# Chunked attention before a mixture of experts: value rows loaded once, 24 rows of each value window copied on chip

## The chip, the cores and the metric

One core of a Trainium2 chip runs the whole program. The metric is the device time in microseconds, from the first to the last instruction of a run; lower is better. The profile is one execution recorded by the hardware profiler; its engines are called PE (TensorE, the matrix engine), DVE (VectorE), ACT (ScalarE), POOL (GpSimd) and SP (the engine that does nothing here but issue loads).

## What is computed

The reference is attention over short windows, followed by a layer of experts of which each token uses one:

```python
B, H, S, D = q.shape                      # 4, 8, 768, 64
chunk, left_ctx, right_ctx = (32, 16, 8)
for c in range(S // chunk):               # 24 chunks
    l_start = max(0, c * chunk - left_ctx)
    r_end = min(S, c * chunk + chunk + right_ctx)
    k_full = np.concatenate([mem_k, k[:, :, l_start:r_end]], axis=2)    # 8 memory rows, up to 56 of the sequence
    v_full = np.concatenate([mem_v, v[:, :, l_start:r_end]], axis=2)
    a = softmax(scale * q_c @ k_full.T)
    out[:, :, c * chunk:c * chunk + chunk] = a @ v_full
x = out.transpose(0, 2, 1, 3).reshape(B * S, H * D)
# gate: each token's expert of 8 and its probability; then
out[mask] = gate_w[mask, None] * (np.maximum(x[mask] @ w1[e], 0) @ w2[e])
```

Consecutive windows overlap: a window has 56 rows of the sequence and the next one starts 32 rows further on, so 24 rows of each window are also in the one before it.

## The kernel before

**Units.** The attention goes through 16 units of two heads each (`NU`), and each unit in two halves of 12 chunks (`hf`). One pass of the loop at L731 is one half unit: it computes the scores of its half (`scores`, L273), the products with the values of the half before (`attend`, L306), and the transposes of the finished half before that (`trans_x`, L328). `trans_k`, `regroup_q` (L228, a VectorE copy of q) and `store_k` (L265) for unit u+1 stand in the first half of unit u, `trans_q` in the second; the values of unit u+1 are first used in the second half of unit u+1, one pass after its first scores.

**The tiles.** `kbds` (two of them) hold the keys of a unit, 64 columns to a chunk and head: 8 memory keys written by `mem_keys` (L247, GpSimd; the first units on VectorE) and 56 of the sequence written by `store_k`. `vws` (three of them, `NVW`) hold the values: partition 64 h + r is row r of the window of head h, the free dimension is chunk, head and 64 + 1 columns. The extra column is 1 for rows that count, so that its product is the softmax's denominator; rows outside the sequence have 0 there, from `vmask`. The tiles are blanked once at the start (`blank_v`, L205, L208, L210).

**The loads.** All loads of q, k and v are issued by SP, in the order of the program: `load_qk` (L96) three units ahead and `load_v` (L219 to L223) two units ahead, at the end of the first half of a unit. A value load may start when the products that used the same tile three units before are done. Per head there are four loads: memory rows for all 24 chunks (rows 0 to 7), 56 rows for the 22 inner chunks, 40 rows for the first and 48 for the last. Each moves rows of 64 numbers, 256 B.

**Other queues.** Instructions of TensorE, SP and GpSimd run in the order of the program. GpSimd has the memory keys, the store of each finished unit to the tensor `xd` (L333, a DMA), the store of the gates (L497), and some one-hot rows of the routing (L558, L560: tiles 0 and 1 of batches 0, 1 and 2). The routing of a batch of tokens (`route`) is cut into small steps that `pump` puts between the attention's instructions; TensorE multiplies the one-hot rows (L568) at its place in the order. After the last unit, the weights of the experts stream in (`load_w`, L600, L604), are split into two parts (`conv`, L607, L608) and multiplied (L650, L662).

Of the kernel before, what the change touches and what calls it, by code (L numbers as in the profile page):

```python
# [48 lines left out]
def tile_chunk_attention_top1_moe(  # L49
# [47 lines left out]

    # the tensor engine's clock comes up while the first loads are on their way
    idle = const.tile([P, 640], BF16, name="idle")
# [10 lines left out]

    # ---------------------------------------------------------------- constants
    kbds = [pers.tile([P, NCH, 2, 64], F32, name=f"kbd{i}") for i in range(2)]
# [28 lines left out]
    nc.gpsimd.iota(iota_i, [[1, 192]], base=0, channel_multiplier=0)  # L141
    # rows of a value window that lie outside the sequence
    kcol = const.tile([P, 1], F32, name="kcol")
# [3 lines left out]
    mtmp = const.tile([P, 1], F32, name="mtmp")  # L147
    nc.gpsimd.tensor_scalar(vmask[:, 0:1], kcol, 23.5, None, op0=ALU.is_gt)
    nc.gpsimd.tensor_scalar(mtmp, kcol, 7.5, None, op0=ALU.is_lt)
    nc.gpsimd.tensor_add(vmask[:, 0:1], vmask[:, 0:1], mtmp)  # L150
    nc.gpsimd.tensor_scalar(vmask[:, 1:2], kcol, 55.5, None, op0=ALU.is_lt)

# [21 lines left out]
    def more_constants():  # L174
        nc.vector.tensor_copy(iota, iota_i)
        nc.vector.tensor_scalar(rev[:, 0], iota[:, 0:E], -1.0, float(E), op0=ALU.mult, op1=ALU.add)
        nc.vector.memset(ones_b, 1.0)
        nc.vector.tensor_scalar(tri_b, iota[:, 0:P], pcol, None, op0=ALU.is_gt)
        # EMPTY less the token number, and its negative, for token T*128+p
        nc.vector.tensor_scalar(tokn, iota[:, 0:N // P], float(P), pcol, op0=ALU.mult, op1=ALU.add)  # L180
        nc.vector.tensor_scalar(tokn, tokn, -EMPTY, None, op0=ALU.add)
        nc.vector.tensor_scalar(tokm, tokn, -1.0, None, op0=ALU.mult)
        nc.vector.memset(table, EMPTY)
        nc.vector.tensor_scalar(tail_row, pcol[0:64], 31.5, None, op0=ALU.is_gt)
        nc.vector.tensor_scalar(col0, iota[0:64, 0:E], float(HI), None, op0=ALU.mult)
        nc.vector.memset(tot, 0.0)
        nc.vector.tensor_copy(mod_f, mod_i[:, :, 0])
    def bias_rows():
        # of each token
        modT = bank()  # L190
        nc.tensor.transpose(modT[:, 0:N // P], mod_f, ident[0:N // P, 0:N // P])
        mt = const.tile([P, N // P, 1], F32, name="mt")
        m0 = const.tile([P, N // P, 1], F32, name="m0")
        nc.vector.tensor_copy(mt[:, :, 0], modT[:, 0:N // P])
        nc.vector.tensor_scalar(m0, mt, -1.0, 1.0, op0=ALU.mult, op1=ALU.add)
        bsh = [P, N // P, E]
        b1t = pers.tile(bsh, F32, name="b1t")
        nc.vector.tensor_tensor(btok, m0.to_broadcast(bsh), bias_b[:, 0:1, :].to_broadcast(bsh), op=ALU.mult)
        nc.vector.tensor_tensor(b1t, mt.to_broadcast(bsh), bias_b[:, 1:2, :].to_broadcast(bsh), op=ALU.mult)
        nc.vector.tensor_add(btok, btok, b1t)  # L200

    # ---------------------------------------------------------------- attention
    def blank_v(i):
# [10 lines left out]
    def load_v(u):  # L214
        vw = vws[u % NVW]
        for h in range(2):
            hh = 2 * u + h
            r0 = 64 * h
            nc.sync.dma_start(vw[r0:r0 + NMEM, :, h, 0:D], mvf[hh].unsqueeze(1).to_broadcast([NMEM, NCH, D]))  # L219
            src = bass.AP(tensor=vf.tensor, offset=(hh * S + 16) * D, ap=[[D, 56], [32 * D, NCH - 2], [1, D]])  # L220
            nc.sync.dma_start(vw[r0 + NMEM:r0 + 64, 1:NCH - 1, h, 0:D], src)
            nc.sync.dma_start(vw[r0 + 24:r0 + 64, 0, h, 0:D], vf[hh * S:hh * S + 40])
            nc.sync.dma_start(vw[r0 + NMEM:r0 + 56, NCH - 1, h, 0:D], vf[hh * S + 720:hh * S + S])  # L223

# [19 lines left out]
    def mem_keys(u, eng):  # L244
        for h in range(2):
            r = slice(64 * h, 64 * h + 64)
            eng.tensor_copy(kbds[u % 2][r, :, h, 0:NMEM], memT[r, u:u + 1, :].to_broadcast([64, NCH, NMEM]))  # L247

    def trans_k(u):
        k2 = k2s.pop(u)  # L250
        for h in (1, 0):
            hh = 2 * u + h
            t = kts[u, h] = bank()
            for i in range(3):
                nc.tensor.transpose(t[:, 8 + i * P:8 + (i + 1) * P], k2[:, 3 * h + i, :], ident)
            # memory keys stand where the first and last windows pass the sequence's ends
            pads = bass.AP(tensor=t.tensor, offset=t.offset, ap=[list(t.ap[0]), [392, 2], [1, 8]])
            mem_sel = ident[:, 4 * hh:4 * hh + 4].unsqueeze(1).unsqueeze(1)
            nc.tensor.matmul(pads, mkp, mem_sel.to_broadcast([P, 2, 2, 4]), start=True, stop=True)  # L259

    def store_k(u, h, j, copy):
        tt = kts[u, h][64 * j:64 * j + 64]
        win = bass.AP(tensor=tt.tensor, offset=tt.offset, ap=[list(tt.ap[0]), [16, NCH], [1, 28]])
        dst = kbds[u % 2][64 * h:64 * h + 64, :, h, NMEM:64]
        copy(dst.rearrange("p c (i j) -> p c i j", j=2)[:, :, :, j], win)  # L265
# [68 lines left out]

    # the routing of a batch goes on between the instructions of the attention
    routing, now = [], [0]
# [15 lines left out]

    # ---------------------------------------------------------------- routing, in stages
    plan = {}
# [11 lines left out]
    def plan_row(pos, tail, pt, nfull):  # L366
        """For the slot that stands at pos: its expert, whether that is new, its first column of the table."""
        vec = nc.vector
# [8 lines left out]
        if tail is not None:  # L377
# [5 lines left out]
            vec.tensor_add(three[:, 2], three[:, 2], c)  # L383
            # a tail that follows a slot of its own expert
            vec.tensor_tensor(same, pos, nfull, op=ALU.is_equal)
# [7 lines left out]
    def plan_slots():  # L393
        """Slots of 256 tokens of one expert, those of expert ohg first."""
        vec = nc.vector
# [5 lines left out]
        vec.tensor_tensor_scan(end, oth, oth, ng, op0=ALU.add, op1=ALU.bypass)  # L401
        # first slot and the one behind the last; of expert ohg, 0 and its number of slots
        vec.tensor_sub(sta, end, oth)
# [7 lines left out]
    def plan_tails():  # L411
        """Behind the slots, tails of up to 128 against the order of the experts, that of expert ohg last.

        Row p of regs holds slot p for p < 32, tail p - 32 from there on."""
        vec = nc.vector
# [20 lines left out]
    def route(b):  # L436
# [24 lines left out]
        yield "v"  # L461
        # first expert of those with the largest logit
        eq = sm.tile(sh, F32, name="eq")
# [12 lines left out]
        yield "pe"  # L476
        # rank of each token within its expert, and the counts
        rkb = bank()
# [7 lines left out]
        nc.tensor.matmul(rkf[:, 0:NT * E], tri_b, oh.rearrange("p t e -> p (t e)"), start=False, stop=True)  # L486
        # gate
        sx = sm.tile([P, NT, 1], F32, name="sx")
# [28 lines left out]
        if b == B - 2:  # L517
            # the expert with the most tokens so far has at least one full slot
            cm = sm.tile([P, 1], F32, name="cm")
# [19 lines left out]
        if b == B - 1:  # L539
            nc.vector.tensor_copy(plan_new("counts"), rk[0:64, NT, :])  # L540
            yield "v"
        # where the token goes: row lo, column ac of the table
        hot = []
# [33 lines left out]

    # ---------------------------------------------------------------- experts
    raw, wh, wl = [None] * 16, [None] * 16, [None] * 16
# [65 lines left out]
    def mm1(f):  # L645
        ph = bank()[:, 0:256]
        # what waits for the lower part of x comes last
        for n in range(12):
# [25 lines left out]

    # the same for up to 128 tokens, whose products have the tokens on the partitions
    def tail_mm1(half):
# [27 lines left out]

    # ---------------------------------------------------------------- the run
    for i in range(NVW):
# [16 lines left out]
    for i in range(1, NVW):  # L723
        load_v(i)

    units = [(u, hf) for u in range(NU) for hf in range(2)]
# [4 lines left out]
    for i in range(n + 2):  # L731
# [12 lines left out]
        if u + 1 < NU and hf == 0:  # L744
# [10 lines left out]
            pump(1)  # L755
        elif u + 1 < NU:
            trans_q(u + 1)
            store_q(u + 1, 0)
            store_q(u + 1, 1)
            exps(u, hf)  # L760
            pump(3)
        elif live:
            exps(u, hf)
            pump(3)
# [34 lines left out]
        if (u, hf) == (NU - 2, 1):  # L799
# [13 lines left out]
            gather(0)  # L813
            # the later weights wait for the gather to be under way
            for f in range(NFIRST, 8):
# [126 lines left out]
```

## Time and profile before

| | |
|---|---|
| runs (three) | median 504.73 us, 500.7 to 508.09 |
| the profiled execution | span 505.4 us, mean granted TensorE clock 0.954 |
| busy over the span | PE 454.4 us, DVE 335.7, ACT 296.1, POOL 145.9 |
| DMA | 104448 packets, 64.48 MB; 53851 packets under 512 B |
| first product with values to the last | 22.3 to 170.6 us |
| first weights of the experts issued | 161.8 us |

How to read it: rows of busy time by window give, after the window and its length, the busy time of PE, PEld (TensorE's weight load), DVE, ACT and POOL with the number of instructions in brackets, then the granted TensorE clock, the share of time the 16 DMA engines were busy on average, and the GB/s moved. Rows in order of time give start and duration in us, the engine, the line, the operation with its tiles, and in square brackets how long the engine sat idle and what ended that. Groups of instructions give the total busy time in us and the mean in ns, then the idle time before them. Rows of waits give the total, the number and the longest. DMA issues give KB for one DMA.

### The profile page before, as it was taken

To read this page: it belongs to the slowest core of one execution; us is meant where nothing else is said; L and a number is where in the kernel's file an instruction comes from. 1 tells how busy PE (TensorE), PEld (TensorE's weight loads), DVE (VectorE), ACT (ScalarE), POOL (GpSimd) and SP (SyncE) were. 2 spreads that over 40 slices of the span, in tenths; PEclk is the share of its full clock that TensorE was granted. 3 is DMA by queue.
4 is the path that set the end of the run, shared out by engine and by line. 5 is a ranking of instruction groups with operands and counts; after the bars stand their busy time and mean duration, and the time that the engine had idled before them with its cause. 6 is when DMAs were issued, how large, how long until landed. Compare 5 with 4: busy or idle time off the path is not lost. (4 is left out here: it accounts for less than half of the span.)

```text
span 505.4 us, 12069 instructions
## 1 busy us (share of the span) xinstructions
PE 454.4 (90%) x4093; PEld 387.5 (77%) x4093; DVE 335.7 (66%) x760; ACT 296.1 (59%) x588; POOL 145.9 (29%) x238
## 2 busy tenths in 40 slices
PE   6769878796788779899999999999999999999892
PEld 3657666585666568889898989898898989897672
DVE  7756675584768597576865758484756657575593
ACT  5457674583655655546465656464655656565682
POOL 8112115114215582403051625343030303030100
PEclk8699997897999998999999999999999999999897
DMA  8999989989999921202031368771111202020830
GB/s 176 167 214 181 204 170 211 213 178 177 185 212 188 330 89 22 86 22 83 2 99 29 106 169 272 231 243 64 43 58 28 84 1 85 1 85 5 263 117 10
DMA packets 104448, 64.48 MB, mean 128 GB/s; under 512 B 53851, under 2 KB 95027, under 8 KB 104372
## 3 DMA queue, kind: packets, MB, share of 16 engines
q1 hardware_dynamic: 96512, 41.76, 38.9%
q0 software_dynamic: 6720, 21.62, 14.0%
q8 instruction: 36, 0.59, 0.5%
q14 instruction: 40, 0.33, 0.2%
q10 hardware_dynamic: 1140, 0.18, 0.2%
HBM read 97.05 MB, written 13.16 MB: 218 GB/s over the span
## 5 line engine op out<-in xcount | busy, mean ns | idle before, releaser
L650 PEld LDWEIGHTS tr<-xt,w 128*128 128x128 f32 x1152 | 141.2, 193 | 2.4 <-issue 0.6
L650 PE MATMUL tr<-xt,w 128*128 128x256 f32 x1152 | 142.7, 285 | 0.2 <-DVE h L652 0.2
L608 DVE TENSOR_TENSOR wl<-raw,wh 128x512 fp32r<-128x512 f32 x107 | 76.7, 727 | 13.9 <-ACT wh L607 5.9
L608 DVE TENSOR_TENSOR w<-raw,w 128x512 fp32r<-128x512 f32 x115 | 72.5, 686 | 0.0
L667 POOL DMA_INDIRECT out_dram<-o,ix_now x24 | 24.3, 1013 | 165.3 <-ACT o L666 161.6
L662 PE MATMUL av<-wh,h 128*128 128x512 f32 x208 | 69.9, 402 | 0.0
L662 PE MATMUL sc<-wh,h 128*128 128x512 f32 x208 | 69.7, 402 | 0.0
L607 ACT CAST w<-raw 128x512 fp32r<-128x512 f32 x120 | 66.9, 625 | 4.5 <-DMA raw<-in_moe_w_dram 4.5
L607 ACT CAST wh<-raw 128x512 fp32r<-128x512 f32 x112 | 67.2, 613 | 2.4 <-DVEq L907 2.2
L651 ACT ACTIVATE h<-tr 128x256 fp32r<-128x256 f32 x96 | 36.6, 383 | 48.3 <-PE tr L650 31.8
L652 DVE SCALAR_TENSOR_TENSOR h<-tr,h 128x256 fp32r<-128x256 f32 x96 | 40.7, 424 | 35.3 <-ACT h L651 35.2
L642 ACT CAST xt<-tr 128x512 fp32r<-128x512 f32 x26 | 15.1, 587 | 68.8 <-PE tr L640 46.6
L643 DVE TENSOR_TENSOR xt<-tr,xt 128x512 fp32r<-128x512 f32 x26 | 17.8, 692 | 52.9 <-ACT xt L642 52.9
L306 PE MATMUL av<-vw,PT 128*32 128x130 f32 x768 | 32.1, 295 | 17.8 <-DMA k<-in_k_dram 7.5
L662 PEld LDWEIGHTS av<-wh,h 128*128 128x128 f32 x208 | 39.2, 189 | 9.1 <-DVE h L703 0.4
L662 PEld LDWEIGHTS sc<-wh,h 128*128 128x128 f32 x208 | 39.0, 188 | 9.1 <-DVE h L703 0.4
L265 ACT COPY kbd<-tr 64x672 f32<-64x672 f32 x47 | 36.2, 769 | 15.1 <-PE tr L259 14.6
L662 PE MATMUL av<-wl,h 128*128 128x512 f32 x104 | 41.0, 394 | 0.0
L662 PE MATMUL sc<-wl,h 128*128 128x512 f32 x104 | 40.9, 393 | 0.0
L306 PEld LDWEIGHTS av<-vw,PT 128*32 128x32 f32 x768 | 23.0, 116 | 21.7 <-issue 11.6
L333 POOL DMA_DIRECT2D xd<-xb x16 | 14.0, 876 | 73.8 <-DVE l L453 29.8
L273 PE MATMUL sc<-kbd,qT 128*32 128x128 f32 x768 | 30.1, 294 | 4.5 <-DVE kbd L265 4.5
(206 smaller groups left out, 645.8 us busy)
## 6 DMA issues: line engine op xcount, KB each, us to landing
raw<-in_moe_w_dram SPq DMA_DIRECT2D x240, 256.0 KB
vw<-in_v_dram SPq DMA_DIRECT2D x32, 308.0 KB
k<-in_k_dram SPq DMA_DIRECT2D x16, 384.0 KB
q<-in_q_dram SPq DMA_DIRECT2D x16, 384.0 KB
xd<-xb POOLq DMA_DIRECT2D x16, 384.0 KB, 6.7
vw<-in_mem_v_dram SPq DMA_DIRECT2D x32, 48.0 KB
vw<-in_v_dram SPq DMA_DIRECT2D x32, 10.0 KB
vw<-in_v_dram SPq DMA_DIRECT2D x32, 12.0 KB
```

Of the source, the lines that this page charges most:

```text
L265: copy(dst.rearrange("p c (i j) -> p c i j", j=2)[:, :, :, j], win)
L273: nc.tensor.matmul(sc[32 * j:32 * j + 32, t * P:(t + 1) * P], qT[:, 32 * c:32 * c + 32], kbd[:, c].rearrange("p h m -> p (h m)"), start=Tr ...
L306: nc.tensor.matmul(avb[32 * j:32 * j + 32, t * W:(t + 1) * W], PT[:, t * P + 32 * j:t * P + 32 * j + 32], vw[:, c].rearrange("p h d -> p ( ...
L607: nc.scalar.copy(wh[i], raw[i])
L608: (eng or nc.vector).tensor_sub(wl[i], raw[i], wh[i].bitcast(F32))
L642: nc.scalar.copy(xth[:, sl], t)
L643: nc.vector.tensor_sub(xtl[:, sl], t, xth[:, sl].bitcast(F32))
L650: nc.tensor.matmul(ph, w[f][:, c * P:(c + 1) * P], x[:, c, :], start=(n == 0), stop=(n == 11))
L651: nc.scalar.activation(hh[:, f], ph, AF.Relu)
L652: nc.vector.scalar_tensor_tensor(hl[:, f], ph, 0.0, hh[:, f].bitcast(F32), op0=ALU.max, op1=ALU.subtract)
L662: nc.tensor.matmul(pos[t], x, w[8 + f], start=(f == 0 and n == 0), stop=(f == 7 and n == 2))
L667: return nc.gpsimd.indirect_dma_start(out=out, out_offset=bass.IndirectOffsetOnAxis(ap=ix, axis=0), in_=o, in_offset=None, bounds_check=N ...
```

## The change

The order of the rows in a window is turned round: rows 0 to 55 are the sequence, 56 to 63 the memory (keys and values alike, masks accordingly). Of the sequence, `load_v` loads only what the chunk before does not have: rows 24 to 55 of chunks 0 to 22, rows 24 to 47 of the last chunk, and rows 16 to 23 of the first. The memory rows are loaded last of the four instead of first. Rows 0 to 23 of chunks 1 to 23 are copied by GpSimd from rows 32 to 55 of the chunk before, in the same tile: one copy a head (`share_v`), 24 partitions by 23 x 64 numbers. These copies stand behind the first value loads for unit 0, and for unit u+1 at the start of the second half of unit u, ahead of `trans_q`.

```diff
-    nc.gpsimd.tensor_scalar(vmask[:, 0:1], kcol, 23.5, None, op0=ALU.is_gt)
-    nc.gpsimd.tensor_scalar(mtmp, kcol, 7.5, None, op0=ALU.is_lt)
-    nc.gpsimd.tensor_add(vmask[:, 0:1], vmask[:, 0:1], mtmp)
-    nc.gpsimd.tensor_scalar(vmask[:, 1:2], kcol, 55.5, None, op0=ALU.is_lt)
+    nc.gpsimd.tensor_scalar(vmask[:, 0:1], kcol, 15.5, None, op0=ALU.is_gt)
+    nc.gpsimd.tensor_scalar(vmask[:, 1:2], kcol, 47.5, None, op0=ALU.is_lt)
+    nc.gpsimd.tensor_scalar(mtmp, kcol, 55.5, None, op0=ALU.is_gt)
+    nc.gpsimd.tensor_add(vmask[:, 1:2], vmask[:, 1:2], mtmp)
...
-            nc.sync.dma_start(vw[r0:r0 + NMEM, :, h, 0:D], mvf[hh].unsqueeze(1).to_broadcast([NMEM, NCH, D]))
-            src = bass.AP(tensor=vf.tensor, offset=(hh * S + 16) * D, ap=[[D, 56], [32 * D, NCH - 2], [1, D]])
-            nc.sync.dma_start(vw[r0 + NMEM:r0 + 64, 1:NCH - 1, h, 0:D], src)
-            nc.sync.dma_start(vw[r0 + 24:r0 + 64, 0, h, 0:D], vf[hh * S:hh * S + 40])
-            nc.sync.dma_start(vw[r0 + NMEM:r0 + 56, NCH - 1, h, 0:D], vf[hh * S + 720:hh * S + S])
+            src = bass.AP(tensor=vf.tensor, offset=(hh * S + 8) * D, ap=[[D, 32], [32 * D, NCH - 1], [1, D]])
+            nc.sync.dma_start(vw[r0 + 24:r0 + 56, 0:NCH - 1, h, 0:D], src)
+            nc.sync.dma_start(vw[r0 + 24:r0 + 48, NCH - 1, h, 0:D], vf[hh * S + S - 24:hh * S + S])
+            nc.sync.dma_start(vw[r0 + 16:r0 + 24, 0, h, 0:D], vf[hh * S:hh * S + 8])
+            nc.sync.dma_start(vw[r0 + 56:r0 + 64, :, h, 0:D], mvf[hh].unsqueeze(1).to_broadcast([NMEM, NCH, D]))
+
+    def share_v(u):
+        vw = vws[u % NVW]
+        for h in range(2):
+            r0 = 64 * h
+            nc.gpsimd.tensor_copy(vw[r0:r0 + 24, 1:NCH, h, 0:D], vw[r0 + 32:r0 + 56, 0:NCH - 1, h, 0:D])
...
-            eng.tensor_copy(kbds[u % 2][r, :, h, 0:NMEM], memT[r, u:u + 1, :].to_broadcast([64, NCH, NMEM]))
+            eng.tensor_copy(kbds[u % 2][r, :, h, 56:64], memT[r, u:u + 1, :].to_broadcast([64, NCH, NMEM]))
...
-        dst = kbds[u % 2][64 * h:64 * h + 64, :, h, NMEM:64]
+        dst = kbds[u % 2][64 * h:64 * h + 64, :, h, 0:56]
...
     for i in range(1, NVW):
         load_v(i)
+    share_v(0)
...
         elif u + 1 < NU:
+            share_v(u + 1)
             trans_q(u + 1)
```

## The prediction

> **What bounds the kernel now.** The page first, to see in which stage the edited lines run and what is full there.
>
> ```profile
> span 505.4 us, 12069 instructions
> ...
> PEclk8699997897999998999999999999999999999897
> DMA  8999989989999921202031368771111202020830
> ```
>
> Forty slices of 12.6 us. DMA is at 8 or 9 tenths for the first fourteen (to about 175 us: the attention) and mostly below 4 behind; in those slices the granted clock dips too. Next the busy times by window: the whole attention loop, then three short stretches.
>
> ```profile
> 16.00:171.00 155.00, 129.12 (x2084) 101.78 (x2076) 101.98 (x309) 95.80 (x184) 39.00 (x67) 0.92 1.01 198
> 33.00:36.00 3.00, 0.49 (x3) 0.52 (x4) 0.48 (x1) 0.00 (x0) 0.00 (x0) 0.91 1.16 304
> 38.00:42.00 4.00, 4.00 (x77) 3.02 (x72) 2.34 (x6) 2.99 (x6) 1.48 (x3) 0.89 0.80 106
> ```
>
> Over the loop the DMA share is 1.01, TensorE is busy 129.12 of 155 us, VectorE 101.98, GpSimd 39.00. The stretch with q and k rows moves 304 GB/s; the one with value rows 106 GB/s, at a share of 0.80. Value rows are the slow traffic. Is the DMA stream what sets the pace? The SP queue in order of time:
>
> ```profile
> 42.80 0.43 SPq L96 DMA_DIRECT2D k<-in_k_dram  x1
> ...
> 44.37 1.59 SPq L221 DMA_DIRECT2D vw<-in_v_dram  x1
> 46.01 2.72 SPq L222 DMA_DIRECT2D vw<-in_v_dram  x1
> 48.78 0.33 SPq L223 DMA_DIRECT2D vw<-in_v_dram  x1
> ...
> 145.75 0.42 SPq L96 DMA_DIRECT2D k<-in_k_dram  x1
> ```
>
> SP issues without a gap, and a 10 KB load (L222) holds it 2.72 us behind the 308 KB load of L221: the stream is pushed back, and SP waits for room rather than for the compute engines. From unit 5's k (42.80) to unit 15's (145.75) are ten units: 10.30 us each. The compute engines need less. TensorE's score blocks, and the wait in the list that follows:
>
> ```profile
> 63.48 0.86 PE L273 MATMUL sc<-kbd,qT 128*32 128x128 f32 x24
> ...
> 67.69 0.86 PE L273 MATMUL sc<-kbd,qT 128*32 128x128 f32 x24
> ...
> 69.92 0.87 PE L306 MATMUL av<-vw,PT 128*32 128x130 f32 x24
> ...
> 71.40 0.86 PE L273 MATMUL sc<-kbd,qT 128*32 128x128 f32 x24
> ...
> 77.53 1.65 PE L306 MATMUL av<-vw,PT 128*32 128x130 f32 x24 [3.19 <-DMA k<-in_k_dram]
> ```
>
> Two unstalled half units take 4.21 and 3.71 us, 7.92 us a unit, routing included. Then comes a stall on a load, and the next block runs 1.65 us instead of the 0.87 us at 69.92. The sums of such waits in the loop:
>
> ```profile
> DVE qr L228 <- DMA q<-in_q_dram: 8.3, 4, 3.1
> ...
> PE av L306 <- DMA k<-in_k_dram: 7.5, 2, 4.3
> ...
> PE av L306 <- DMA vw<-in_v_dram: 5.6, 3, 2.7
> ```
>
> So the attention is paced by its loads; from 171 us on TensorE paces, and nothing there is edited.
>
> **The change, part by part.** The rows per load come from the DMA issues:
>
> ```profile
> vw<-in_v_dram SPq DMA_DIRECT2D x32, 308.0 KB
> k<-in_k_dram SPq DMA_DIRECT2D x16, 384.0 KB
> q<-in_q_dram SPq DMA_DIRECT2D x16, 384.0 KB
> xd<-xb POOLq DMA_DIRECT2D x16, 384.0 KB, 6.7
> vw<-in_mem_v_dram SPq DMA_DIRECT2D x32, 48.0 KB
> vw<-in_v_dram SPq DMA_DIRECT2D x32, 10.0 KB
> vw<-in_v_dram SPq DMA_DIRECT2D x32, 12.0 KB
> ```
>
> *Fewer value rows.* A value row is 256 B. A head now loads 1232 + 192 + 40 + 48 = 1512 of them; after the change 32 x 23 + 24 + 8 + 192 = 960, so a unit of two heads drops from 3024 to 1920, or 276 of its 756 KB. SP still issues four loads a head. Three prices for a unit:
> - By bytes: k, q, xd and values are 1908 KB a unit; 276 / 1908 x 10.30 = 1.5 us.
> - By packets, all alike: k, q and xd have 2304 of 512 B; 1104 / 5328 x 10.30 = 2.1 us.
> - By the stretches: at 304 GB/s the 1152 KB (1.18 MB) of k, q and xd take 3.9 us, the values the other 6.4 us; 1104 / 3024 of it is 2.3 us.
>
> I take 2.0 us, nearest to the packet price, because the 106 GB/s stretch shows that value rows cost more than their bytes. A loss is excluded: the same rows go to the same places, only fewer of them. The new DMA pace is 8.3 us, still above the 7.92 us of the engines. The ten units between the two quoted k issues gain, and with them the values of units 14 and 15, issued after 145.75; the first units meet a pipeline that is still filling, and I count nothing for them. 12 x 2.0 = 24 us.
>
> The Trainium skill, "DMA: Bandwidth & Descriptors", the paragraph "How many engines (k)", says that a DMA runs on the largest number up to 16 that divides its outer dimension. By it the 56-row load has 14 engines and the 32-row load 16, the memory rows 8 before and after. The busiest engine would fall from 382 to 290 packets a unit, an estimate of 7.8 us of DMA. No row here shows single engines; it would lead to the fourth rival below.
>
> *Two copies a unit on GpSimd* (24 partitions, 23 x 64 = 1472 elements). No row shows a copy that moves partitions. The nearest rows:
>
> ```profile
> L247 POOL COPY kbd<-memT 64x192 f32<-64x192 f32 x28 | 10.4, 372 | 8.3 <-PE sc L273 7.1
> L205 POOL MEMSET vw<- 128x3120 f32 x3 | 8.2, 2729 | 0.1
> L608 POOL TENSOR_TENSOR w<-raw,w 128x512 fp32r<-128x512 f32 x5 | 6.7, 1371 | 4.9 <-ACT w L607 4.9
> ...
> L333 POOL DMA_DIRECT2D xd<-xb x16 | 14.0, 876 | 73.8 <-DVE l L453 29.8 <-DVE table L569 11.3 <-DVE xb L321 11.1
> ```
>
> The memset's 0.875 ns an element gives 1.3 us, L608's 2.68 ns gives 3.9 us. L247 is the one plain copy: 372 less 192 x 0.875 leaves 0.2 us fixed. I take 0.2 + 1.3 = 1.5 us, 3.0 us a unit. GpSimd then does 3.0 + 2 x 0.37 + 0.88 = 4.6 of 8.3 us: hidden behind the loads. At 3.9 us it does 9.4 us: that cover is gone, and the pace is 9.4 instead of 8.3, 13 us of the 24 given back.
>
> *The new wait.* The copies of unit u+1 stand in GpSimd's queue at the start of the second half of unit u, and wait for its values to land. Behind them queue the xd store of unit u-1, the memory keys of unit u+2 (needed a unit later), and in the last unit the first gather of the experts' tokens. GpSimd's queue now, from its last one-hot rows to that gather:
>
> ```profile
> 156.82 1.16 POOL L560 TENSOR_SCALAR a<-iota,ac,tokm 128x192 fp32r<-128x192 f32 x1
> 157.94 0.94 POOL L333 DMA_DIRECT2D xd<-xb  x1
> 161.21 0.18 POOL L620 CAST ix<-table 128x2 int32 x1 [2.33 <-DVE table L569]
> ```
>
> The routing's one-hot rows stand ahead of the copies (the steps that issue them run a half unit earlier), so TensorE does not wait for them; the copies of unit 15 come between that one of 156.82 and the store at 157.94. Unit 15's last value load is the last of the stream:
>
> ```profile
> 160.64 0.33 SPq L223 DMA_DIRECT2D vw<-in_v_dram  x1
> ```
>
> With today's backlog the copies would end after about 161 + 3 = 164 us, and the gather, at 161.21 now, would be 3 us late. Where loads set the pace, values land just ahead of their product, and the copies put 3.0 us between; in the stream of units that is only an offset, since the loads of later units go on, and I see it once, at the end: 3 us. Between 0 (loads that have caught up) and 6 (offset and gather one after the other).
>
> *Start.* Unit 0's copies follow the value tiles' memsets and its loads. The value tile's list:
>
> ```profile
> L306 PE MATMUL av<-vw,PT x768: 270/274/427, 22.3 to 170.6; 128*32 128x130 f32 x192
> ...
> L208 POOL MEMSET vw<- x6: 135/138/431, 6.5 to 13.4; 64x24 f32 x6
> ```
>
> Between the last memset (13.4 us) and the first product (22.3) there is room for 3.0 us of copies, unless the loads land late. Nothing to 2 us; I take 1.
>
> *The port between VectorE and GpSimd.*
>
> ```profile
> 7.17 2.70 POOL L205 MEMSET vw<- 128x3120 f32 x1
> ...
> 7.39 2.60 DVE L175 CAST iota<-iota_i 128x192 f32<-128x192 int32 x1
> ```
>
> The one copy of each unit that has the form of this cast, from the loop's groups:
>
> ```profile
> L228 DVE COPY qr<-q 128x768 f32<-128x768 f32 x15 | 8.3, 554 | 8.3 <-DMA q<-in_q_dram 8.3
> ```
>
> A VectorE cast of 192 elements lasts until the memset on GpSimd is over, five times what a copy of 768 (L228) takes. Such a lock could hold VectorE up to two copies a unit, 3.0 us, at L228. VectorE is busy 101.98 / 155 x 10.30 = 6.8 us a unit: with a typical 0.7 us it stays below 8.3. I cost it at nothing; covered by the loads.
>
> The Trainium skill, "SBUF — State Buffer", section "Who interferes with whom", calls this port pair an exclusive lock that the engine which comes first holds for a whole instruction. The two rows above agree, 2.60 us against 2.70; it speaks against the change and is the first rival below.
>
> *Nothing:* the shift of memory keys and masks to other columns has the same instructions with the same shapes; memory rows last instead of first moves 48 KB behind 192 KB in the same queue, no more work.
>
> **Sum:** 505.4 - 24 + 3 + 1 = 485.4 us of span. The runs' median, 504.73, is 0.7 us below the profiled span; so 485 us, its own range 477 to 494.
>
> **Rivals.**
> - *VectorE becomes the bound.* If both copies are in its way in each unit, VectorE needs 6.8 + 3.0 = 9.8 us a unit: 12 x 0.5 = 6 us gained, 499. For it: the locked cast. Against: one SBUF-to-SBUF copy a unit, mostly at another time.
> - *Only the waits for value loads go.* The waits above put just 5.6 us at vw; if the rest of the loop's idle time has other causes, 505.4 - 5.6 + 4 - 0.7 = 503 us. For it: that list. Against: one queue carries all loads, and q and k stand in it behind values.
> - *Slower: the copy that moves partitions is dear.* Place: GpSimd's queue. GpSimd has 1.62 us of other work a unit, so it decides from (10.30 - 1.62) / 2 = 4.3 us a copy; at 5 us the pace is 11.6, 15 x 1.3 = 20 us lost, 525. For it: no row of its kind, and L608 already at 3.9. Against: L247.
> - *The loads stop being the bound.* DMA falls below 7.92 and the engines set the pace: 12 x 2.38 = 29 us, less 1 at the start: 477. For it: the 0.80 share in the value stretch, that is idle DMA engines. Against: no sign yet that the engines hold 7.92 through every unit.
>
> **How the numbers follow.** Forecast 0.54, VectorE 0.12, only the waits 0.12, dear copy 0.10, engines' pace 0.12. Two per cent, 10 us, is about what a measurement of this kernel can tell from no change (its runs spread from 500.7 to 508.09). Faster: 0.54 + 0.12 + 0.03 of VectorE's case = 0.69; same: 0.09 + 0.11 = 0.20; slower: 0.10 + 0.01 = 0.11. Range 473 to 508: from 4 us below the engines' pace, if the first units gain too, to a cheap gain with 4 us of cost behind it (503 and its spread of 4); the dear copy is left out.
>
> **What would show it.** Right: k issues about 8.3 us apart, stalls on k, q and vw loads nearly gone, copies near 1.5 us, the last attention product some 20 us earlier than 171, and the stages behind as long as now. Wrong: copies over 3 us; TensorE waiting for the GpSimd copies; VectorE's L228 at 2 us instead of 0.554; k issues still 10 us apart with a full DMA share, which would say that rows are not what the loads cost.

## The result and the profile after

The changed kernel takes 490.96 us (median of four runs, 488.23 to 491.6), the kernel before 504.67 us in the four runs beside it (500.7 to 508.09). The ratio is 0.973, 95% interval 0.967 to 0.979: faster by some 14 us. The profiled execution took 490.55 us.

The page of the changed kernel, the rows that answer to those of before:

```profile
span 488.8 us, 12153 instructions
...
PEclk9799999999979899999999999999999999999897
DMA  8999999999649202111122578842020202020920
```

The full stretch of DMA ends after ten slices (122 us) instead of fourteen (176 us), and the granted clock dips less in the attention. The whole attention loop by window (columns as before):

```profile
16.00:158.00 142.00, 128.79 (x2125) 99.53 (x2116) 121.64 (x319) 101.35 (x195) 87.75 (x103) 0.96 0.97 194
```

TensorE is now busy 91% of the loop (128.79 of 142; before 129.12 of 155), VectorE 121.64 us, 20 us more than before, GpSimd 87.75 instead of 39.00. The SP queue, unit 5's and unit 15's k and the last of the value loads:

```profile
34.37 0.39 SPq L96 DMA_DIRECT2D k<-in_k_dram  x1
...
115.42 0.39 SPq L96 DMA_DIRECT2D k<-in_k_dram  x1
...
127.01 0.30 SPq L224 DMA_DIRECT2D vw<-in_mem_v_dram  x1
```

8.11 us a unit instead of 10.30. The value tile, first its products and then the copies; behind it the one wait of a compute engine for a load of q, k or v that is left in the loop's list of waits:

```profile
L314 PE MATMUL av<-vw,PT x768: 271/274/423, 21.6 to 152.4; 128*32 128x130 f32 x192
...
L231 POOL COPY vw<-vw x32: 1403/1436/1562, 13.6 to 137.4; 24x1472 f32<-24x1472 f32 x32
```

```profile
POOL vw L231 <- DMA vw<-in_v_dram: 39.5, 19, 4.1
```

The last product comes at 152.4 us, 18.2 us earlier; a copy takes 1.44 us; what waits for values is GpSimd. From the last product to the end it is 336.4 us (488.8 - 152.4), before 334.8: 1.6 us are given back there.

One table reads the traces of the next sections together (the changed kernel's second execution is that of the next section). "Per unit" is the time from the first to the last product over 15.5 units; the next column is the span's rest behind the last product.

| kernel | k of units 5, 15 | a unit, by k | first, last product | per unit | rest |
|---|---|---|---|---|---|
| before | 42.80, 145.75 | 10.30 | 22.3, 170.6 | 9.57 | 334.8 |
| changed | 34.37, 115.42 | 8.11 | 21.6, 152.4 | 8.44 | 336.4 |
| changed, second execution | 35.76, 119.96 | 8.42 | 21.6, 155.4 | 8.63 | 336.9 |
| changed, no copies | 35.69, 117.82 | 8.21 | 21.9, 145.9 | 8.00 | (321.8) |
| changed, half of the 32 rows | 35.94, 114.83 | 7.89 | 22.2, 151.1 | 8.32 | (323.8) |
| before, plus copies | 39.46, 141.35 | 10.19 | 21.6, 176.5 | 9.99 | 336.2 |

In brackets: values that are left out change which expert a token goes to, and these two kernels have one part less to do in the experts' stage (TensorE has 4033 matmuls of 4093). For them, and for the two with 49 and 48 rows, the attention alone is compared.

### The profile page after: what moved, and what is told of

Same layout as the page of the kernel before. It is cut to its first block, busy times and chain, and to the rows that moved or that the text cites. A ratio compares the mean times of both kernels' runs of the same rounds, so it can differ in the third digit from the quotient of the medians.

```text
span 488.8 us, 12153 instructions
## 1 busy us (share of the span) xinstructions
PE 447.9 (92%) x4093; PEld 380.5 (78%) x4093; DVE 353.9 (72%) x760; ACT 296.2 (61%) x588; POOL 192.3 (39%) x270
## 5 line engine op out<-in xcount | busy, mean ns | idle before, releaser
L616 DVE TENSOR_TENSOR wl<-raw,wh 128x512 fp32r<-128x512 f32 x107 | 79.0, 748 | 14.2 <-ACT wh L615 6.8
L660 DVE SCALAR_TENSOR_TENSOR h<-tr,h 128x256 fp32r<-128x256 f32 x96 | 40.7, 424 | 32.9 <-ACT h L659 27.7
L231 POOL COPY vw<-vw 24x1472 f32<-24x1472 f32 x32 | 45.9, 1434 | 40.3 <-DMA vw<-in_v_dram 39.5
L273 ACT COPY kbd<-tr 64x672 f32<-64x672 f32 x47 | 36.2, 770 | 10.3 <-PE tr L267 9.7
L631 POOL DMA_INDIRECT xg<-xd,gx x26 | 28.5, 1094 | 10.6 <-POOL gx L629 6.7
L314 PE MATMUL av<-vw,PT 128*32 128x130 f32 x768 | 28.3, 280 | 2.3 <-ACT PT L304 1.7
```

What stands on the lines that cost most here:

```text
L231: nc.gpsimd.tensor_copy(vw[r0:r0 + 24, 1:NCH, h, 0:D], vw[r0 + 32:r0 + 56, 0:NCH - 1, h, 0:D])
L314: nc.tensor.matmul(avb[32 * j:32 * j + 32, t * W:(t + 1) * W], PT[:, t * P + 32 * j:t * P + 32 * j + 32], vw[:, c].rearrange("p h d -> p ( ...
L616: (eng or nc.vector).tensor_sub(wl[i], raw[i], wh[i].bitcast(F32))
L631: nc.gpsimd.indirect_dma_start(out=xg[t], out_offset=None, in_=xd[0:rows], in_offset=bass.IndirectOffsetOnAxis(ap=gx[:, t:t + 1], axis=0))
L660: nc.vector.scalar_tensor_tensor(hl[:, f], ph, 0.0, hh[:, f].bitcast(F32), op0=ALU.max, op1=ALU.subtract)
```

## What the copies cost

The theory was that loads no longer pace the attention, and that the copies take time by holding VectorE and by keeping GpSimd's queue; the rival, that they are hidden. Four kernels ran side by side. The first is the changed kernel once more.

> The changed kernel once more, beside its variants, so that differences of a few us are read on one chip. Every theory: 488 to 492 us, ratio to the kernel before 0.967 to 0.979.

It took 493.34 us (490.91 to 494.08; ratio 0.981, interval 0.976 to 0.986), just above what was expected. Its last product comes at 155.4: the changed kernel's own last product varies by 3 us. In this execution, not in the first, TensorE waited for memory keys:

```profile
77.55 1.51 PE L281 MATMUL sc<-kbd,qT 128*32 128x128 f32 x24 [2.93 <-POOL kbd L255]
```

**No copies** (rows 0 to 23 of the windows of chunks 1 to 23 keep what the blanking left):

```diff
-            nc.gpsimd.tensor_copy(vw[r0:r0 + 24, 1:NCH, h, 0:D], vw[r0 + 32:r0 + 56, 0:NCH - 1, h, 0:D])
+            pass
```

> The changed loads without the copies on GpSimd: rows 0 to 23 of chunks 1 to 23 are left as they are, so this part of the values is missing. Theory (the copies hold the port that VectorE shares with GpSimd, and VectorE's routing steps stand on the path): 4 to 8 us below the changed kernel, 483 to 487, and VectorE's busy time back near 336 us from 354. Rival (the copies are hidden, the engines' own pace is the bound): within 1.5 us of the changed kernel.

The last product comes at 145.9 us: the copies cost the attention 6.5 us against 152.4, 9.5 against 155.4. The total, 468.75 us (ratio 0.930, 0.924 to 0.936), lies far below the expected 483 to 487; about 15 us of that is the missing part of the experts' stage. TensorE still waited for a load of k here, 2.8 us in two places, so this kernel doesn't show the pace of the engines alone. **Copies twice** (each copy written a second time, the same bytes):

```diff
+            for _ in range(2):
-            nc.gpsimd.tensor_copy(...)
+                nc.gpsimd.tensor_copy(...)
```

> Each copy on GpSimd is made twice, the same bytes again. Theory (port): 4 to 9 us above the changed kernel, 495 to 500, VectorE's busy time up by another 10 to 18 us. Rival (copies hidden): within 1.5 us; GpSimd would have 7.5 of 8.1 us a unit to do, still under the pace.

503.65 us (ratio 1.001, 0.997 to 1.005), 10.3 us above its neighbour of 493.34, last product at 164.3. The second dose cost 9 to 12 us, more than the 4 to 9 expected, and VectorE's busy time rose from 353.9 to 365.7 us: copies of 3 us a unit are not hidden, and doubling them eats the whole gain.

Where they take it is seen at unit 15's copies. Changed kernel, in order of time:

```profile
135.71 0.28 DVE L566 TENSOR_SCALAR l<-iota,lo 128x128 fp32r<-128x128 f32 x1
135.90 1.55 DVE L568 TENSOR_SCALAR a<-iota,ac,tokm 128x192 fp32r<-128x192 f32 x1
135.93 2.90 POOL L231 COPY vw<-vw 24x1472 f32<-24x1472 f32 x2
...
137.37 1.54 DVE L566 TENSOR_SCALAR l<-iota,lo 128x128 fp32r<-128x128 f32 x1
...
138.83 0.37 DVE L568 TENSOR_SCALAR a<-iota,ac,tokm 128x192 fp32r<-128x192 f32 x1
...
139.25 1.62 PE L576 MATMUL tr<-a,l 128*128 128x192 f32 x3 [1.39 <-DVE a L568]
...
140.81 1.51 PE L281 MATMUL sc<-kbd,qT 128*32 128x128 f32 x24
```

VectorE's one-hot rows of the last batch routed in the loop take 1.55 and 1.54 us while GpSimd copies, 0.28 and 0.37 us ahead and behind; TensorE waits for them. TensorE then pays a second time: the clock granted to it is 0.50 from 139 to 145 us (1.00 from 132 to 136), and the block of score products takes 1.51 us, where without copies it takes 0.86 at this place. The step from the products of one half unit to the next is 9.7 us here (starts at 135.3 and 145.0), 4.7 us without copies, 12.2 us with the copies made twice; in the second execution of the changed kernel it is 9.7 us again. **Copies in six** pieces of 256 numbers, so that VectorE can get in between:

```diff
+            for c in range(0, NCH - 1, 4):
+                e = min(c + 4, NCH - 1)
+                nc.gpsimd.tensor_copy(vw[r0:r0 + 24, c + 1:e + 1, h, 0:D], vw[r0 + 32:r0 + 56, c:e, h, 0:D])
```

> Each copy is cut into six of 4 chunks (256 elements, about 0.4 us each), so that GpSimd works somewhat longer in all but holds the port in short pieces. Theory (port): VectorE waits shorter, 2 to 5 us below the changed kernel, 486 to 489. Rival (the products wait for the copies, or the copies are hidden): no gain, 0 to 3 us above.

It took 491.46 us (ratio 0.979, 0.973 to 0.986), as the changed kernel: the expected gain missed. VectorE's busy time fell as the theory has it (341.9 us over the span, 353.9 in the changed kernel) and the long half unit shrank from 9.7 to 5.7 us. But the pieces keep GpSimd longer, 4.33 us for a pair instead of 2.90, and what stands behind them comes later:

```profile
137.97 4.33 POOL L233 COPY vw<-vw 24x256 f32<-24x256 f32 x12
143.22 0.18 POOL L630 CAST ix<-table 128x2 int32 x1
```

```profile
PE sc L283 <- POOL kbd L257: 5.1, 2, 2.6
```

The gather starts 1.6 us later than in the changed kernel (143.22 against 141.58), and TensorE waits 5.1 us for memory keys that stand behind the pieces, in two places; in the changed kernel that wait is absent in one execution and 2.9 us in the other. The last product comes at 153.2. So what was saved on VectorE was lost, and waits behind GpSimd's queue are where the trace shows a loss; that they are all of it is not shown.

## Where the copies stand in GpSimd's queue

**Memory keys ahead**: the keys of unit u+2 are written ahead of the copies of unit u+1, not behind them.

```diff
-            if u > 0:
-                mem_keys(u + 1, nc.gpsimd)
...
         elif u + 1 < NU:
+            if u + 2 < NU:
+                mem_keys(u + 2, nc.gpsimd)
             share_v(u + 1)
```

> The changed kernel with the memory keys of unit u+2 written ahead of the copies of unit u+1 in GpSimd's queue, instead of behind them. Theory now (the copies cost through GpSimd's queue: at the ends of the routing batches the keys come late and the scores wait for them, 2.5 to 3 us each time; and through the port at the last batch): no wait of the scores for the keys is left, 1 to 5 us below the changed kernel, 488 to 492 where it runs at 493. Rival (port alone): within 1 us of it.

488.12 us (487.62 to 494.44; ratio 0.977, 0.971 to 0.983), last product at 151.1, no wait for memory keys left, as expected; but its ratio is not told apart from the changed kernel's. **Last copies late**: unit 15's copies behind the gather.

```diff
-            share_v(u + 1)
+            if u + 2 < NU:
+                share_v(u + 1)
...
             load_w(0, 0)
+            share_v(NU - 1)
```

> The changed kernel with the copies of unit 15 behind the first gather of the experts' tokens, instead of ahead of the last routing steps. Theory: the half unit of 9.7 us there (VectorE's one-hot rows blocked by the two copies, then the gather late) falls to about 5, 3 to 5 us below the changed kernel, 488 to 490. Rival (the copies cost evenly in every unit, so the last ones cost a sixteenth): within 1 us.

495.91 us (ratio 0.989, 0.985 to 0.993), no gain. The long half unit did fall, 9.7 to 5.1 us, but the products of unit 15 now wait for the copies instead:

```profile
145.81 2.89 POOL L231 COPY vw<-vw 24x1472 f32<-24x1472 f32 x2 [2.62 <-issue]
148.76 1.52 PE L314 MATMUL av<-vw,PT 128*32 128x130 f32 x22 [5.63 <-POOL vw L231]
```

Both edits together:

> Both moves together. Theory: they are different places, so they add up, 4 to 9 us below the changed kernel, 484 to 489, and the last product with values near the 146 us that it has with no copies at all. Rival (the engines' pace limits either alone): no better than the better of the two.

490.26 us (ratio 0.978, 0.973 to 0.983), last product at 156.4 instead of near 146: no sum of gains. The last try goes the other way, with the keys ahead: unit 15's copies a half unit **earlier**.

```diff
         if u + 1 < NU and hf == 0:
+            if u == NU - 2:
+                share_v(NU - 1)
             trans_k(u + 1)
```

> The changed kernel with the memory keys of unit u+2 ahead of the copies of unit u+1, and with unit 15's two copies moved a half unit earlier, to the start of the first half of unit 14, ahead of GpSimd's one-hot rows of the last batch instead of behind them. Theory (what the copies cost is their place on GpSimd: they hold VectorE's one-hot rows, and they keep memory keys and the gather waiting): unit 15's values land before 131 us, so nothing new waits; the copies run at about 131 to 134.5, VectorE's last two one-hot rows fall from 1.5 to 1.6 us back to 0.3 to 0.5, GpSimd's own one-hot rows come up to 2.9 us later, which TensorE sees as a wait of 1 to 2 us for them; the longest half unit falls from 9.7 to 7 to 8.5 us, the gather is issued 2 to 3 us earlier, the last product ends at 148 to 150 us (151.1 with the keys ahead alone), and the time is 484 to 487 us. Rival (GpSimd's queue is full at this place, and an order only chooses who waits, as with unit 15's copies behind the gather): the one-hot rows late by 3 us, last product at 151 to 154, time 488 to 491.

The attention did nearly what the theory said: VectorE's one-hot rows are back at 0.27 to 0.43 us but for one of 0.69, the gather starts at 138.28, the longest half unit falls to 8.6 us, the last product comes at 149.1. The time did not: 493.98 us (ratio 0.980, 0.976 to 0.985). The profiled execution was the shortest of its six, 490.13 us; in it the rest behind the last product is 339.3 us instead of 336.4. TensorE and VectorE in order of time, then GpSimd:

```profile
163.95 1.51 PE L459 MATMUL tr<-ident,lgs 128*128 128x128 f32 x6 [7.52 <-DVE h L660]
```

```profile
153.10 10.37 DVE L616 TENSOR_TENSOR wl<-raw,wh 128x512 fp32r<-128x512 f32 x1 [0.61 <-ACT wh L615]
163.40 0.41 DVE L660 SCALAR_TENSOR_TENSOR h<-tr,h 128x256 fp32r<-128x256 f32 x1
```

```profile
153.06 3.77 POOL L616 TENSOR_TENSOR w<-raw,w 128x512 fp32r<-128x512 f32 x3
156.78 6.14 POOL L616 TENSOR_TENSOR wl<-raw,wh 128x512 fp32r<-128x512 f32 x5
```

VectorE splits weights beside GpSimd, which splits eight tiles without a gap from 153.06 to 162.92. VectorE's one subtraction, of a kind that takes 0.75 us on average (107 of them in the changed kernel), ends only after the last of the eight. The next step of the activation (L660, also on VectorE) queues behind it, and TensorE stands for 7.52 us. In the changed kernel the same place reads so, VectorE, GpSimd and TensorE:

```profile
156.35 6.52 DVE L616 TENSOR_TENSOR wl<-raw,wh 128x512 fp32r<-128x512 f32 x1 [0.87 <-ACT wh L615]
```

```profile
156.14 3.74 POOL L616 TENSOR_TENSOR w<-raw,w 128x512 fp32r<-128x512 f32 x3
159.84 2.47 POOL L616 TENSOR_TENSOR wl<-raw,wh 128x512 fp32r<-128x512 f32 x2
```

```profile
163.26 2.93 PE L658 MATMUL tr<-xt,w 128*128 128x256 f32 x12 [4.88 <-DVE h L660]
```

4.88 us of wait behind five such tiles; 3.13 us with the keys ahead, 1.39 us with the last copies late; before, 0.17 us. The rest behind the last product is 339.3 us where this wait is 7.52, 336.4 where it is 4.88, 335.4 with the keys ahead and 331.3 with the last copies late. It doesn't simply follow how early the attention is done: with the copies made twice the last product comes at 164.3, and yet the wait is 4.37 us and the rest 337.3. Nor is the wait all of the rest: before has nearly none of it and a rest of 334.8. That the wait makes the rest longer is read from the traces; no run took it away, and what sets its length is not shown. The interval of each of these orders overlaps at least one of the changed kernel's two, so none of them is shown to beat it.

## What sets the pace after the change

**Half of the rows**: 16 instead of 32 rows in the load of the chunks' own rows (rows 40 to 55 of these windows, and what is copied from them, keep what the blanking left).

```diff
-ap=[[D, 32], [32 * D, NCH - 1], [1, D]])
+ap=[[D, 16], [32 * D, NCH - 1], [1, D]])
```

> The changed kernel with 16 instead of 32 rows in the main value load; the other 16 rows of each window are missing, so the routing and with it the experts' stage differ, and only the attention is compared, by the last product with values (152.4 and 155.4 us in the two profiles of the changed kernel). Theory (the engines and GpSimd's queue set the pace now): between 147 and 155 us. Rival (loads still set the pace): 1.3 us a unit less, 133 to 138 us.

736 rows a unit less (16 x 23 x 2), and the last product comes at 151.1 us, 1.3 us earlier than in the changed kernel's first execution and 4.3 earlier than in its second (in total 476.76 us, with the smaller experts' stage). In the changed kernel the loads no longer set the pace; if they had, the rival's 133 to 138 us was due.

**The copies in the kernel before**, into a spare tile that nobody reads, at the same place of GpSimd's queue:

```diff
+            nc.gpsimd.tensor_copy(spare[r0:r0 + 24, 1:NCH], vw[r0 + 32:r0 + 56, 0:NCH - 1, h, 0:D])
```

> The kernel before, with all its loads, plus the same two copies a unit at the same place of GpSimd's queue, into a spare tile that nobody reads. Theory (copies cost time only where the loads no longer set the pace): k issues stay 10.2 to 10.5 us apart, the last product comes 0 to 3 us later than 170.6, and the time is 0 to 4 us longer, most of it at the last batch and the gather. Rival (the copies cost their 6 to 9 us by the port and the queue whatever sets the pace): last product at 176 to 180, time 6 to 9 us longer, 511 to 514.

513.99 us (ratio 1.015, 1.009 to 1.022), 9 us longer, the last product at 176.5 us. My theory, that slow loads would cover the copies, fell; the rival's numbers held. Its waits say why:

```profile
POOL spare L231 <- DMA vw<-in_v_dram: 73.1, 27, 6.0
...
PE sc L281 <- POOL kbd L255: 12.3, 7, 4.0
```

GpSimd stands 73.1 us waiting for values, and the memory keys stand behind those waits: TensorE loses 12.3 us to them, in seven places. An example, GpSimd's queue and then TensorE's:

```profile
60.74 1.41 POOL L231 COPY spare<-vw 24x1472 f32<-24x1472 f32 x1 [4.13 <-DMA vw<-in_v_dram]
63.42 1.44 POOL L231 COPY spare<-vw 24x1472 f32<-24x1472 f32 x1 [1.27 <-DMA vw<-in_v_dram]
64.81 0.83 POOL L341 DMA_DIRECT2D xd<-xb  x1
65.68 0.73 POOL L255 COPY kbd<-memT 64x192 f32<-64x192 f32 x2
```

```profile
66.47 0.86 PE L281 MATMUL sc<-kbd,qT 128*32 128x128 f32 x24 [1.52 <-POOL kbd L255]
```

The wait for the memory keys is dearer the later the values come: 12.3 us here, where loads pace, none and 2.9 us in the two executions of the changed kernel. Part of the 12.3 us is covered, since the last product moves by 5.9 us.

## What a row costs

Two kernels change only how many of the 56 rows the inner load of the kernel before takes.

```diff
-ap=[[D, 56], [32 * D, NCH - 2], [1, D]])
+ap=[[D, 49], [32 * D, NCH - 2], [1, D]])
```

> The kernel before with 49 instead of 56 rows in the load of the 22 inner chunks (rows 57 to 63 of the inner chunks' windows keep what the blanking left: the computation lacks them, and the routing behind it differs, so that the stretch up to the last attention product is what counts). Theory (a load costs by its rows): 308 of 3024 value rows a unit are gone; by the 10.30 and 8.11 us a unit of the kernels before and after, 1104 rows apart, a row costs 2.0 ns, so k issues 9.7 us apart and the last product 7 to 10 us earlier than 170.6, at 160 to 164. The Trainium skill, DMA: Bandwidth & Descriptors, the paragraph How many engines (k), would put 49 rows on 7 engines, where 56 rows go on 14: by that page the busiest engine goes from 382 to 514 packets a unit, an estimate of k issues near 13.9 us apart and a last product past 200 us.

With 308 rows a unit less, the attention is slower: k issues from 46.61 to 162.21, 11.56 us a unit, last product at 189.7. The rows theory (9.7, 160 to 164) is out. (514.75 us in total, ratio 1.021, in spite of the smaller experts' stage.) The Trainium skill, "DMA: Bandwidth & Descriptors", "How many engines (k)", puts a load of 49 rows on 7 engines; the estimate made from that, by packets on the busiest engine, has the sign right and the size too large (13.9 us).

> The kernel before with 48 instead of 56 rows in the load of the 22 inner chunks: one row less than in the run with 49 (rows 56 to 63 of the inner chunks' windows keep what the blanking left: the computation lacks them, and only the stretch up to the last attention product counts). With 49 rows k issues came 11.56 us apart, with 56 rows 10.30. Theory (rows cost 2.0 ns each as long as they go over many DMA engines, and with 49 it was the few engines that set the pace): 352 of 3024 rows a unit are gone, 0.7 us; k issues 9.4 to 9.8 us apart, last product at 156 to 163 us. Rival one (the busiest engine sets the pace in the kernel before too): by 338 instead of 382 packets on it, counted by the rule that the Trainium skill, DMA: Bandwidth & Descriptors, gives under How many engines (k), an estimate of 9.1 us, last product at 150 to 156. Rival two (the loss with 49 rows has nothing to do with how rows divide over engines, but with any load cut short): k issues still 11 us apart or more.

One row less again, and k issues are 10.19 us apart (43.70 to 145.57), the last product at 171.9: as the kernel before, with 352 rows a unit less (493.94 us in total, by the smaller experts' stage); the 0.11 us between 10.30 and 10.19 is less than the 0.31 us between the two executions of the changed kernel. None of the three expectations held. The load queue between 44 and 114 us (packets, MB, share of 16 engines), first of the kernel before:

```profile
q1 hardware_dynamic: 32124, 10.75, 82.7%
```

Of the kernel with 49 rows:

```profile
q1 hardware_dynamic: 26219, 8.90, 58.6%
```

Of the kernel with 48 rows:

```profile
q1 hardware_dynamic: 29188, 10.00, 92.8%
```

Of the changed kernel:

```profile
q1 hardware_dynamic: 31368, 11.30, 88.0%
```

Engine time per packet is 70 us x 16 x share / packets: 28.8, 25.0, 35.6 and 31.4 ns. With 49 rows, this queue leaves four tenths of the engines' time while the loads are late, as if few engines carried them; no row shows single engines. With 48, the queue fills 92.8%, but a packet takes 24% longer, and that eats the rows saved. Why it does so stays open. The changed kernel's 31.4 ns is not like for like: 44% of the packets of q, k and v are of 512 B there, 34% in the kernel before. So that the new loads freed the attention is shown, but not whether by their fewer rows alone or also by how they divide.

## Why the prediction was right, and where it wasn't

The time, 485 us forecast and 490.96 measured, and the sign are right; so are the cause (loads pace the kernel before, and the new loads free it) and most sizes. The state that was forecast is not the one that came, and the agreement of the largest term is in part luck: it took 2.0 us for 12 units, where the products give 1.57 us a unit (9.57 less 8.00 without copies) for all 15.5 units, 24.3 us. The 6 us by which the time was missed are 1.8 us of the attention (18.2 us earlier instead of 20), 1.6 us behind it, and 2.5 us in the step from the profile to the median.

- **Fewer value rows, 24 us.** The attention without copies ends 24.7 us before that of the kernel before (170.6 - 145.9). The size is right; its working is not. "The new DMA pace is 8.3 us, still above the 7.92 us of the engines" fails: k issues came 8.11 us apart (8.42 in the second execution), but half the rows moved the last product by 1.3 us only, so it is not the loads that hold the changed kernel at 8.44 us a unit. That is the state of the fourth rival, given 0.12. Whether the engines alone would hold 7.92 is not shown: without copies it is 8.00, with 2.8 us of waits for k in it.
- **The packet price, 2.1 us.** It counts 768 packets of 512 B a unit for the stores to `xd`. Their queue in the kernel before (row below, 44 to 114 us, seven such stores) has 856 packets, some 122 a store; with these the price is 1104 / 4682 x 10.30 = 2.4 us.

```profile
q0 software_dynamic: 856, 2.87, 14.6%
```

- **A price per row.** "A loss is excluded: ... only fewer of them" fails as reasoning: by k issues 308 rows fewer lost 1.26 us a unit, 352 fewer gained next to nothing (0.11), 1104 fewer gained 2.19 (1.88 in the second execution). The time of a load does not follow from the number of its rows alone.
- **The first units, counted at nothing.** Unit 5's k came 8.4 us earlier (42.80 to 34.37), ten units more gave 21.9, so unit 15's k moved by 30.3 us. Of this 12.1 us only made the loads lead: from that k to the last product it is 37.0 us, before 24.85. What is left is the 18.2 us. k issues are the pace of the loads; the pace of the attention must be read from its products.
- **The copies' own time**, 1.5 us: 1.44. Memory keys and masks, start (first product 21.6, before 22.3): as forecast or better than the 1 us allowed.
- **"Hidden behind the loads", 3 us at the end.** Mis-sized: 6.5 us (9.5 in the other execution). The gather was not late: it starts at 141.58, and TensorE, which transposes the gathered rows (L648) just ahead of the last product, did not wait for them, where it waited 1.1 us before. The cost sat in the last routed batch, 3.8 us (a step of 9.7 and one of 2.3 us where there are 4.7 and 3.5 without copies), and in half units scattered over the loop.
- **"The port ... I cost it at nothing; covered by the loads"** is the step that failed. The cover was gone with the loads' pace. VectorE's copy of q (the row below) took 762 ns instead of 554, not the 2 us that I had named as the sign; the one-hot rows of the routing, which I had not looked at, went from 0.37 to 1.55 us at unit 15's copies, and TensorE waited 2.3 us for those. VectorE as a bound (499 us) did not come: 121.64 of 142 us.

```profile
L236 DVE COPY qr<-q 128x768 f32<-128x768 f32 x15 | 11.4, 762 | 0.0
```

- **"Memory keys of unit u+2 (needed a unit later)"** fails when values are late: the copies wait for the landing, and only a half unit is left then. It cost 2.9 us in one execution of the changed kernel, none in the other, 12.3 us in the kernel before with copies.
- **"The stages behind as long as now"**: 1.6 us longer by the traces. One wait there grew by 4.7 us (0.17 to 4.88), where GpSimd's weight splits now run without a gap beside VectorE's. It reads like the same lock; no run tests it.
- **From span to median.** Before's profiled execution (505.4) lay 0.7 us above the shown median by its span; runs are some 1.75 us longer than their spans (490.55 and 488.8), so it was a long one, by some 2.5 us. The profiled pair differs by 16.6 us, the medians by 13.7.

Of the rivals, "only the waits for value loads" (503) fell with the 18.2 us, the dear copy (525) with 1.44 us.

## What to carry to other kernels

When a change frees the bound that covered its own cost, cost that cost against the next bound: here the copies were hidden only on paper, since with the loads gone from the path, what held VectorE or stood ahead of other work on GpSimd counted. On GpSimd's in-order queue, ask for each new wait what stands behind it and when that is needed counted from the end of the wait, not from its issue. Read a pace from the instructions that finish the work: loads that come early only lead.

## What the runs showed of the hardware

- A copy of 24 partitions by 1472 numbers that moves partitions by 32 costs GpSimd 1.44 us, 0.98 ns a number; a pair of them cut into twelve pieces costs 4.33 us against 2.90.
- A VectorE instruction beside GpSimd does not wait for one GpSimd instruction alone: a subtraction of some 0.75 us took 10.37 us and ended behind eight GpSimd instructions in a row. The Trainium skill, "SBUF — State Buffer", "Who interferes with whom", speaks of a lock held for one whole instruction; the measurement goes further than that.
- One row more or less in a load moved the pace of all loads by 1.37 us a unit (49 rows 11.56, 48 rows 10.19), and fewer rows did not mean less time.
- Behind a short stretch with little work TensorE ran at half its clock: in the changed kernel it was busy 0.96 us of the 3 us from 136 to 139, and the granted clock is 0.50 from 139 to 145 us; in the second execution it was busy 1.35 us of 73 to 77.5, and the clock is 0.50 from 77.5 to 83 us.
